# Sums of w3's halves on the tensor engine, and a second-layer group begun inside the last product of its input

## The chip, the cores and the metric

The kernel runs on one core of one Trainium2 chip. The time is device microseconds of that core. Three runs of the kernel before took 1224.52, 1227.14 and 1231.71 us; the median, 1227.14 us, is the time that the change is compared with. The profile is one further execution.

## The reference

Inputs are q, k, v of shape (8, 8, 576, 64) and two feed-forward layers. In short:

```python
# attention inside chunks of 64 tokens, per head
s = q_c @ k_c.T / sqrt(64); a = softmax(s); x = a @ v_c      # -> x: 4608 x 512
# layer 1
h = x @ w_in                 # 512 -> 2048
x = (h * sigmoid(h)) @ w_out # 2048 -> 512
# layer 2
h = x @ w_in2                # 512 -> 1024
e = exp(h - max(h)); solu = h * e / (sum(e) + 1e-9)
ln = (solu - mean) / sqrt(var + 1e-6) * g_ln
out = ln @ w_out2            # 1024 -> 512
```

All of it is float32.

## The kernel before

**Numbers.** Every float32 operand is kept as a float16 high half and a float16 low half (`split`, L105: ACT writes the high half, DVE or POOL the low half as the difference). A product of two operands is three matmuls: high by high, high by low, low by high.

**Blocks.** 4608 tokens are nine blocks of 512 (b = 0 to 8), each four tiles of 128 tokens. Attention of block b+1 is worked beside block b. A block runs in stages on PE (the tensor engine): H, the first layer's hidden values (w1, from x); X, the first layer's output (w2), which is the second layer's input; M, the second layer's hidden values (w3); then O, the output (w4).

**Seven products.** From b = 2 on, H, X and M cut each matrix product into 2 by 2 parts and take seven products in place of eight. Sums of the weights' quarters are wanted for that: w1's and w2's are made in block 1 (`w1_sums`, `w2_sums`, through `pe_sums`: PE adds high and low halves with an identity matrix, ACT and DVE finish), w3's in block 2 (`w3_sums`, L665, through `add_sums`, L368: DVE adds the halves, L371, and makes the sums, L372 to L375). `w3_sums` is called at steps 0 and 3 of block 2's X. `combine` (L486) walks the seven products in the order of its argument `seq`: PE accumulates in PSUM tiles pa, pb, pc; ACT copies some of them out (L496, L500, L503), DVE adds (`add`: L534 for H and X, L710 for M), and `done` is called for each quarter of the result as it is complete. For X, `done` (L596) splits the quarter (x2q), makes the four sums xt for M (L610 to L613), and splits those (x2s).

**Around the end of a block.** X's last product is j = 5, 48 matmuls 128x256 in four quarters of 12, one tile of streamed weights each (`x_product`, L574). The next block begins with M's group c = 0 (`m_fast(b - 1, 0)`; seven products of six matmuls 128x512, L696 to L698; tokens c = 0 want x2q and x2s of column c = 0 only), then its H. Group c = 1 comes in the middle of the next H stage. After M comes `m_norm`: maxima (nm, L749), exponentials (L752), normalisation (L754 to L772), a transposing DMA (L776).

**What sets the order.** The program is written in this order; a scheduler then orders instructions per engine by when they were written and what they need, so work of a later step can stand earlier on an engine. Each engine runs its list strictly in that order. All eight PSUM banks have one tag and go round. w1's and w2's products come through a ring of eight tiles of 256 KB (L440 to L457) that the SP queue loads, one load after each use; the same queue issues q, k and v (L170, L179) and the transposes. Names: q is the split hidden value of H, hc and xc are quarters of H and X, uT is the transposed normalised value, kb and qbh are k and q split for the scores, vbh and vbl the halves of v, s_ps the scores, x_ps the attention output, xf and xd its sums.

Of the kernel before, what the change touches and what calls it, by code (L numbers as in the profile page):

```python
# [12 lines left out]
ALU = mybir.AluOpType  # L13
# [3 lines left out]
P = 128  # L17
# [13 lines left out]
HB = BLK // 2  # L31
# [15 lines left out]
def fused(ctx: ExitStack, tc: tile.TileContext, qkv, w1, w2, w3, w4, g_ln, out):  # L47
    nc = tc.nc
    V, A, G, T = nc.vector, nc.scalar, nc.gpsimd, nc.tensor
# [13 lines left out]
    MO = (0, 1, 2, 3)  # L63
# [18 lines left out]
    for d in range(KD):  # L82
        for f in range(4):
            if f % 2 == 0:
                tag = f"w2_{2 * d + f // 2}" if d < 3 else f"q{12 + f // 2}"
                y = one.tile([P, 2, 2, 4, P], F16, tag=tag, name="w2t")
# [5 lines left out]
    w3q = {(n, k): one.tile([P, 2, 2, 512], F16, tag=f"w3_{n}{k}", name="w3q") for n in range(2) for k in range(2)}  # L92
# [63 lines left out]
    seq = [b * TPB + o for b in range(NB) for o in ORDER]  # L156
# [208 lines left out]

    def add_sums(ys, quads, engs):  # L368
        y11, y12, y21, y22 = ys
        for y, a, eng in zip(ys, quads, engs):  # L370
            eng.tensor_tensor(out=y, in0=a[:, 0], in1=a[:, 1], op=ALU.add)  # L371
        V.tensor_tensor(out=y22, in0=y21, in1=y22, op=ALU.add)  # L372
        V.tensor_tensor(out=y21, in0=y11, in1=y21, op=ALU.subtract)
        V.tensor_tensor(out=y11, in0=y22, in1=y11, op=ALU.subtract)
        V.tensor_tensor(out=y12, in0=y12, in1=y11, op=ALU.subtract)  # L375

    def pe_sums(ys, quads, y1122=None):

        n = 512 // P // quads[0].shape[2]

        def whole(qs):
            ps = [bank([P, n, 512 // n], "wq") for _ in range(len(qs) // n)]
            out = []
            for i, a in enumerate(qs):
                o = ps[i // n][:, i % n]
                for l in range(2):
                    T.matmul(o, ident16, a[:, l].rearrange("p a b -> p (a b)"), start=l == 0, stop=l == 1)
                out.append(o)
            return ps, out

        y11, y12, y21, y22 = (y.rearrange("p a b -> p (a b)") for y in ys)
        ps, o = whole([quads[0], quads[3]])
        if n == 2:
            A.activation(y1122, ps[0], AF.Copy)
        else:
            A.activation(y11, o[0], AF.Copy)
            A.activation(y22, o[1], AF.Copy)
        _, (p21, p12) = whole([quads[2], quads[1]])
        V.tensor_tensor(out=y22, in0=p21, in1=y22, op=ALU.add)
        V.tensor_tensor(out=y21, in0=y11, in1=p21, op=ALU.subtract)  # L400
        V.tensor_tensor(out=y11, in0=y22, in1=y11, op=ALU.subtract)
        V.tensor_tensor(out=y12, in0=p12, in1=y11, op=ALU.subtract)
# [9 lines left out]
            nc.sync.dma_start(out=dst(j), in_=z)  # L412

    sn = [0]
    E3, UL = (V, V, V, V), V

    def w1_sums(p):
        wa, wb = w1t[p], w1t[p + K1 // 2]
# [64 lines left out]
                T.matmul(ps[:, c], wl, x[:, 0, k], start=False, stop=k == 1, skip_group_check=True)  # L483
        ring.load()

    def combine(h, shape, seq, product, done, add):  # L486

        a, c = bank(shape, "pa"), {}
        for j in seq:
            if j == 0:
                product(j, a, True)
                A.activation(h[0], a, AF.Copy)  # L496
            elif j == 3:
                c[0] = bank(shape, "pb")
                product(j, c[0], True)
                A.activation(h[3], c[0], AF.Copy)  # L500
            elif j == 1:
                product(j, a, False)
                A.activation(h[1], a, AF.Copy)  # L503
            elif j == 4:
                p = bank(shape, "pc")
                product(j, p, True)
                add(0, h[0], p)
                done(0, 0, h[0])
            elif j == 2:
                product(j, a, False)  # L510
                add(3, h[3], a)
                done(1, 1, h[3])
            elif j == 6:
                product(j, c[0], False)
                add(1, h[1], c[0])
                if seq[-1] != 5:
                    done(1, 0, h[1])
            else:
                product(j, a, False)
                done(0, 1, a)  # L520
                if seq[-1] == 5:
                    done(1, 0, h[1])
            yield

    def run(*parts):

        parts = list(parts)
        while parts:
            for g in list(parts):
                if next(g, parts) is parts:  # L530
                    parts.remove(g)
# [39 lines left out]

        yield from combine(h, [P, 2, HB], HSEQ, lambda *a: h_product(b, *a), done, plain_add)

    def x_product(b, j, ps, start):  # L574
        for c in range(2):
            for q in range(2):
                w = ring.take()
                for f in range(4):
                    wh, wl = w[:, 0, f], w[:, 1, f]
                    g = qt[b, j, q][:, :, f]  # L580
                    first = start and c + q + f == 0
                    T.matmul(ps[:, c], wh, g[:, 0], start=first, stop=False, skip_group_check=True)  # L582
                    T.matmul(ps[:, c], wh, g[:, 1], start=False, stop=False, skip_group_check=True)  # L583
                    T.matmul(ps[:, c], wl, g[:, 0], start=False, stop=q == 1 and f == 3, skip_group_check=True)  # L584
                ring.load()

    def x_fast(b, step):
        h = [one.tile([P, 2, HB], F32, tag=f"w1_{12 + n}", name=f"xc{n}") for n in range(4)]

        def product(j, ps, start):  # L590
            step(XSEQ.index(j))
            x_product(b, j, ps, start)

        xs = {}

        def done(r, c, x):  # L596

            if (r, c) == (0, 1):
                A.activation(h[2], x, AF.Copy)
                x = h[2]  # L600
            scale = S_X2 / (S_G * S_W)
            n = HB if r else P
            y = one.tile([P, 2, 2, HB], F16, tag=f"x2_{2 * r + c}", name="x2q")
            split(y[:, 0, :, :n], y[:, 1, :, :n], x[:, :, :n], scale, A, V)
            xq[b, r, c] = y
            xs[r, c] = x
            if (0, c) in xs and (1, c) in xs:
                (a1, b1), (a2, b2) = ((xs[i, c][:, :, 0:P], xs[i, c][:, :, P:HB]) for i in range(2))
                t = one.tile([P, 4, 2, P], F32, tag=f"q{8 + c}", name="xt")
                TX.tensor_tensor(out=t[:, 0], in0=b1, in1=a1, op=ALU.subtract)  # L610
                TX.tensor_tensor(out=t[:, 2], in0=b2, in1=b1, op=ALU.subtract)
                TX.tensor_tensor(out=t[:, 1], in0=b2, in1=t[:, 0], op=ALU.subtract)
                TX.tensor_tensor(out=t[:, 3], in0=a2, in1=t[:, 1], op=ALU.subtract)  # L613
                z = [one.tile([P, 4, 2, P], F16, tag=f"w1_{8 + 2 * c + i}", name="x2s") for i in range(2)]
                split(*z, t, scale, A, V)
                xq[b, 2, c] = z

        run(combine(h, [P, 2, HB], XSEQ, product, done, plain_add))

    more_ = lambda b: b + 1 < NB  # L620
    TX = V
# [43 lines left out]
    def w3_sums(k):  # L665

        if not w3s:
            for j, n in ((1, 0), (2, 1), (3, 2), (5, 3)):
                w3s[j] = one.tile([P, 2, 2, 512], F16, tag=f"w2_{n}", name="w3s")
            w3s[0], w3s[4], w3s[6] = w3q[0, 0], w3q[0, 1], w3q[1, 1]  # L670
        ys = [one.tile([P, 2, 512], F32, tag=f"w2_{4 + i}", name="y") for i in range(2)]
        y = [ys[i // 2][:, i % 2] for i in range(4)]
        add_sums(y, [w3q[n, i][:, :, k] for n in range(2) for i in range(2)], E3)
        for i, j in ((0, 1), (3, 2), (2, 3), (1, 5)):
            split(w3s[j][:, 0, k], w3s[j][:, 1, k], y[i], 1.0, A, G)

# [101 lines left out]
    def in_turn(*parts):  # L778
        for g in parts:
            yield from g  # L780
# [120 lines left out]
    for b in range(NB):  # L901
# [4 lines left out]
        for f in range(K1):  # L906
# [22 lines left out]
            elif f % 8 == 0:  # L929
                if f and more:  # L930
                    load_qk(m, ("w1_14", "w1_15"))
                    prep_qk(m, ahead=False)
                if b == FAST:
                    for n in range(2):
                        run(m_h(b - 1, MO[f // 4 + n], *(("m1", "m2"), ("w2_5", "w2_4"))[n % 2]))
                if f and b == FAST:
                    for n in range(2):
                        run(m_out(b - 1, MO[n]))
                elif b > FAST:
                    run(m_fast(b - 1, f // 8), in_turn(*(m_out(b - 1, MO[n]) for n in range(2) if f)))  # L940
                run(h_fast(b, f // 4), h_fast(b, f // 4 + 1))
        if b == 0:
            g_split(b, K1 - 1, GH)
# [37 lines left out]
        if b < FAST:  # L981
            for s in range(8):
                step(s)
                x_part(b, s // 2, s % 2)
        else:
            x_fast(b, step)

    b = NB - 1
    run(m_fast(b, 0, alt=True))
    run(m_fast(b, 1), in_turn(m_out(b - 1, MO[2], high=False), m_out(b - 1, MO[3])))  # L990
    for t in MO:
        run(m_out(b, t))
# [47 lines left out]
```

## Time and profile before

| | before |
|---|---|
| runs (us) | 1224.52, 1227.14, 1231.71 |
| profiled execution (us) | 1232.02 |
| span of the profile (us) | 1230.2 |
| mean granted clock of PE | 0.979 |
| PE busy | 1132.8 us, 92% |
| DVE busy | 915.6 us, 74% |
| ACT busy | 802.5 us, 65% |
| POOL busy | 247.9 us, 20% |

The span is the time from the first to the last instruction; 1.8 us lie around it. A row of the timeline gives a start in us, the duration, the engine, the line, the operation, what it writes and reads, and in brackets how long its engine had stood idle before it and what ended that. PE is the busiest engine, but the shares are means over stages that differ: block 2's X stage (382.6 to 449.8 us) is not like block 3's (519.3 to 572.3 us), though PE has the same products in both. A granted clock of 1.00 is the full 2.4 GHz, 0.50 is 1.2 GHz.

### The profile page before, as it was taken

Reading aid. Unit: us, or ns where it says so; the run is one execution under the profiler, and the core shown is the slowest. Engines: PE = TensorE matmul, PEld = TensorE weight load, DVE = VectorE, ACT = ScalarE, POOL = GpSimd, SP = SyncE. Lnnn points to the kernel's source line nnn. Section 1 sums busy time; section 2 is a strip of 40 time slices with the busy share of each in tenths; the row PEclk is TensorE's granted clock in tenths of the full one; section 3 lists DMA queues with packets and bytes.
Section 4 is the critical chain, followed back from the end, with each engine's and each line's share of the span. In section 5 each row is a group of like instructions: output and inputs, shape, how many; then the busy total and the mean of one; then the engine's idle time right before and its main releaser. Section 6 shows DMA issues by size and latency. Waiting matters only on the chain.

```text
span 1230.2 us, 23553 instructions
## 1 busy us (share of the span) xinstructions
PE 1132.8 (92%) x9020; PEld 768.9 (63%) x9020; DVE 915.6 (74%) x1646; ACT 802.5 (65%) x1471; POOL 247.9 (20%) x241
## 2 busy tenths in 40 slices
PE   4997889988998699998999899999999999999998
PEld 4444334444656567686778676767676667776863
DVE  6788986577677878688868886888688867876353
ACT  7777667676666558755875587558755775677253
POOL 3355423334101510032003200220021002100001
PEclk8898989999999899999999999999999999999999
DMA  8778643543534565666566655665566657764604
GB/s 293 247 242 229 194 131 112 168 137 115 140 114 159 149 177 155 183 195 189 155 180 198 189 155 179 191 197 155 159 210 197 155 134 211 187 154 117 211 26 111
DMA packets 205169, 209.18 MB, mean 170 GB/s; under 512 B 120192, under 2 KB 130432, under 8 KB 205056
## 3 DMA queue, kind: packets, MB, share of 16 engines
q1 hardware_dynamic: 205056, 207.68, 57.8%
q8 instruction: 70, 1.15, 0.4%
q14 instruction: 43, 0.35, 0.1%
HBM read 156.24 MB, written 24.12 MB: 147 GB/s over the span
## 4 chain that ended last, share of the span: by engine, by line
PE 33%; DVE 11%; ACT 5%; DMA 5%; issue 3%; SPq 1%; POOL 0%; POOLq 0%; ACTq 0%
PE o_ps L790 3%; PE o_ps L791 3%; PE o_ps L798 3%; PE pa L584 2%; PE pa L583 2%; PE pa L582 2%; DVE vbl L113 2%; DMA ring<-w1s 2%; PE pa L481 2%; PE pa L483 1%; PE pa L482 1%; SPq L776 1%; ACT u L760 1%; PE pa L696 1%; PE pa L698 1%
## 5 line engine op out<-in xcount | busy, mean ns | idle before, releaser
L113 DVE SCALAR_TENSOR_TENSOR q<-hc,q 128x512 f16<-128x512 f32 x196 | 139.4, 719 | 14.6 <-ACT q L108 13.2
L108 ACT ACTIVATE q<-hc 128x512 f16<-128x512 f32 x196 | 120.9, 626 | 37.2 <-DVE hc L569 12.0
L112 POOL TENSOR_TENSOR qbl<-qk,qbh 64x512 f16<-64x512 f32 x58 | 75.5, 1302 | 253.8 <-ACT qbh L108 207.9
L582 PE MATMUL pa<-q,ring 128*128 128x256 f16 x448 | 123.7, 276 | 0.0
L584 PE MATMUL pa<-q,ring 128*128 128x256 f16 x448 | 123.6, 276 | 0.0
L583 PE MATMUL pa<-q,ring 128*128 128x256 f16 x448 | 123.6, 276 | 0.0
L790 PE MATMUL o_ps<-w4h,uT 128*128 128x512 f16 x288 | 109.3, 379 | 1.7 <-DMA uT<-u 1.7
L791 PE MATMUL o_ps<-w4l,uT 128*128 128x512 f16 x288 | 109.2, 379 | 0.0
L767 POOL TENSOR_TENSOR c<-c,mhalf 128x2 f32<-128x2 f32 (+1 forms) x22 | 14.1, 640 | 426.6 <-DVE c L766 426.6
L482 PEld LDWEIGHTS <-ring 128*128 128x128 f16 x784 | 76.6, 98 | 21.1 <-issue 10.9
L481 PEld LDWEIGHTS <-ring 128*128 128x128 f16 x784 | 76.6, 98 | 18.7 <-DMA ring<-w1s 8.3
L584 PEld LDWEIGHTS <-ring 128*128 128x128 f16 x784 | 77.2, 98 | 9.5
L583 PEld LDWEIGHTS <-ring 128*128 128x128 f16 x784 | 77.2, 98 | 9.2
L582 PEld LDWEIGHTS <-ring 128*128 128x128 f16 x784 | 77.2, 98 | 9.1
L483 PEld LDWEIGHTS <-ring 128*128 128x128 f16 x784 | 76.6, 98 | 9.0
L752 ACT ACTIVATE u<-e,nm 128x1024 f32<-128x1024 f32 x28 | 32.2, 1150 | 59.7 <-DVE nm L749 59.7
L481 PE MATMUL pa<-xb,ring 128*128 128x256 f16 x224 | 61.1, 273 | 10.4 <-DMA ring<-w1s 5.3
L798 PE MATMUL o_ps<-w4h,uT 128*128 128x512 f16 x288 | 70.3, 379 | 0.0
L481 PE MATMUL pa<-x,ring 128*128 128x256 f16 x224 | 61.0, 273 | 4.7 <-ACT hc L496 2.9
L481 PE MATMUL pb<-x,ring 128*128 128x256 f16 x224 | 61.1, 273 | 0.2 <-DMA ring<-w1s 0.2
L582 PE MATMUL pb<-q,ring 128*128 128x256 f16 x224 | 61.1, 273 | 0.0
L584 PE MATMUL pb<-q,ring 128*128 128x256 f16 x224 | 61.1, 273 | 0.0
(268 smaller groups left out, 3511.4 us busy)
## 6 DMA issues: line engine op xcount, KB each, us to landing
ring<-w1s SPq DMA_DIRECT2D x196, 256.0 KB, 3.5
ring<-w2s SPq DMA_DIRECT2D x196, 256.0 KB, 3.8
wst<-w SPq DMA_DIRECT2D x48, 512.0 KB, 4.9
qk<-qkv SPq DMA_DIRECT2D x29, 512.0 KB, 3.8
vs<-qkv SPq DMA_DIRECT2D x36, 256.0 KB, 3.4
out<-o SPq DMA_DIRECT2D x36, 256.0 KB, 2.1
w1s<-ws SPq DMA_DIRECT2D x32, 128.0 KB, 1.8
w2s<-ws SPq DMA_DIRECT2D x16, 256.0 KB, 2.0
```

The source lines that it names most:

```text
L108: A.activation(dst_h, src, AF.Copy, scale=scale)
L112: return G.tensor_tensor(out=dst_l, in0=src, in1=dst_h, op=ALU.subtract).ins
L113: return V.scalar_tensor_tensor(out=dst_l, in0=src, scalar=scale, in1=dst_h, op0=ALU.mult, op1=ALU.subtract).ins
L481: T.matmul(ps[:, c], wh, x[:, 0, k], start=first, stop=False, skip_group_check=True)
L482: T.matmul(ps[:, c], wh, x[:, 1, k], start=False, stop=False, skip_group_check=True)
L483: T.matmul(ps[:, c], wl, x[:, 0, k], start=False, stop=k == 1, skip_group_check=True)
L582: T.matmul(ps[:, c], wh, g[:, 0], start=first, stop=False, skip_group_check=True)
L583: T.matmul(ps[:, c], wh, g[:, 1], start=False, stop=False, skip_group_check=True)
L584: T.matmul(ps[:, c], wl, g[:, 0], start=False, stop=q == 1 and f == 3, skip_group_check=True)
L790: T.matmul(ps, uh[:, k], w4h[:, k, :], start=k == 0, stop=False)
L791: T.matmul(ps, uh[:, k], w4l[:, k, :], start=False, stop=False)
L798: T.matmul(ps, ul[:, k], w4h[:, k, :], start=False, stop=k == K2 - 1)
```

## The change

Two things are changed. First, `w3_sums` uses `pe_sums`: the halves of w3's quarters are added by PE (two identity matmuls per quarter, 16 in all), ACT copies two of the four sums out of PSUM, and DVE makes the other combinations from PSUM and these. The function now takes tiles with or without a fourth dimension (`flat`). Second, `m_fast(b, 0)` is created before X of the same block, and X's last product advances it by one product after each of its four quarters (`beside`); its other three products run where the group stood, at the start of the next block. So that the operands are there, `combine` may call `done` for quarter (1, 0) right after product 6 (`c21_first`), which X does.

```diff
-    def add_sums(ys, quads, engs):
-        y11, y12, y21, y22 = ys
-        for y, a, eng in zip(ys, quads, engs):
-            eng.tensor_tensor(out=y, in0=a[:, 0], in1=a[:, 1], op=ALU.add)
-        V.tensor_tensor(out=y22, in0=y21, in1=y22, op=ALU.add)
-        V.tensor_tensor(out=y21, in0=y11, in1=y21, op=ALU.subtract)
-        V.tensor_tensor(out=y11, in0=y22, in1=y11, op=ALU.subtract)
-        V.tensor_tensor(out=y12, in0=y12, in1=y11, op=ALU.subtract)
+    def flat(a, keep):
+        if len(a.shape) == keep + 1:
+            return a
+        return a.rearrange("p l a b -> p l (a b)" if keep == 2 else "p a b -> p (a b)")
...
     def pe_sums(ys, quads, y1122=None):
-        n = 512 // P // quads[0].shape[2]
+        ys, quads = ([flat(a, k) for a in v] for v, k in ((ys, 1), (quads, 2)))
+        n = 512 // quads[0].shape[2]
...
-                    T.matmul(o, ident16, a[:, l].rearrange("p a b -> p (a b)"), start=l == 0, stop=l == 1)
+                    T.matmul(o, ident16, a[:, l], start=l == 0, stop=l == 1)
...
-    def combine(h, shape, seq, product, done, add):
+    def combine(h, shape, seq, product, done, add, c21_first=False):
...
             elif j == 6:
                 product(j, c[0], False)
                 add(1, h[1], c[0])
-                if seq[-1] != 5:
+                if c21_first:
                     done(1, 0, h[1])
             else:
                 product(j, a, False)
                 done(0, 1, a)
-                if seq[-1] == 5:
+                if not c21_first:
                     done(1, 0, h[1])
...
-    def x_product(b, j, ps, start):
+    def x_product(b, j, ps, start, beside=()):
...
                 ring.load()
+                next(iter(beside), None)
...
-    def x_fast(b, step):
+    def x_fast(b, step, beside):
...
-            x_product(b, j, ps, start)
+            x_product(b, j, ps, start, beside if j == XSEQ[-1] else ())
...
-        run(combine(h, [P, 2, HB], XSEQ, product, done, plain_add))
+        run(combine(h, [P, 2, HB], XSEQ, product, done, plain_add, c21_first=True))
...
-        add_sums(y, [w3q[n, i][:, :, k] for n in range(2) for i in range(2)], E3)
+        pe_sums(y, [w3q[n, i][:, :, k] for n in range(2) for i in range(2)])
...
-                    run(m_fast(b - 1, f // 8), in_turn(*(m_out(b - 1, MO[n]) for n in range(2) if f)))
+                    run(m_fast(b - 1, 1) if f else begun, in_turn(*(m_out(b - 1, MO[n]) for n in range(2) if f)))
...
-            x_fast(b, step)
+            begun = m_fast(b, 0, alt=not more)
+            x_fast(b, step, begun)
...
-    run(m_fast(b, 0, alt=True))
+    run(begun)
```

DVE's list in block 2's H stage, before: the first sums of w3 (L371, L372) stand between the last normalisation of block 1 (L772) and the adds of the H quarters (L534).

```order
L772 TENSOR_TENSOR u<-e,u 128x1024
L371 TENSOR_TENSOR y<-w3q 128x512 x2
L372 TENSOR_TENSOR y<-y 128x512
L534 TENSOR_TENSOR hc_3931<-pc,hc_3931 128x512
L534 TENSOR_TENSOR hc_3951<-pc,hc_3951 128x512
L534 TENSOR_TENSOR hc_3934<-pa,hc_3934 128x512
L113 SCALAR_TENSOR_TENSOR q<-hc_3931,q 128x512
L113 SCALAR_TENSOR_TENSOR q<-hc_3951,q 128x512
```

The same place now (line numbers of the changed kernel are up to two lower; L532 is the add of H quarters):

```order
L770 TENSOR_SCALAR e<-e,nmu,c 128x1024
L772 TENSOR_TENSOR u<-e,u 128x1024
L532 TENSOR_TENSOR hc_3931<-pc,hc_3931 128x512
L532 TENSOR_TENSOR hc_3951<-pc,hc_3951 128x512
L532 TENSOR_TENSOR hc_3934<-pa,hc_3934 128x512
L113 SCALAR_TENSOR_TENSOR q<-hc_3931,q 128x512
L113 SCALAR_TENSOR_TENSOR q<-hc_3951,q 128x512
```

The three instructions on w3 have left this place; DVE's first operation of the new sums (L397) stands behind the last split of q.

PE's list at the end of block 2's X now: after the second quarter of X's last product (L580 to L582, accumulating in pa) comes the second M product (L696 to L698, into pb), then X's third quarter.

```order
L582 LDWEIGHTS ring
L582 MATMUL pa<-q,ring 128x256
L696 LDWEIGHTS x2s
L696 MATMUL pb<-w3s,x2s 128x512
L697 LDWEIGHTS x2s
L697 MATMUL pb<-w3s,x2s 128x512
L698 LDWEIGHTS x2s
L698 MATMUL pb<-w3s,x2s 128x512
...
L580 LDWEIGHTS ring
L580 MATMUL pa<-q,ring 128x256
```

Before, all 48 matmuls of X's last product stood ahead of the first M product. Of M's seven products the first four (0, 3, 1, 4) now stand after X's first, second, third and last quarter, and 2, 6 and 5 behind them.

DVE's list at the end of block 3's X, before (x2s in the last row but two is the low half of the sums for c = 0):

```order
L612 TENSOR_TENSOR xt<-xc_5916,xt 128x256
L113 SCALAR_TENSOR_TENSOR x2q<-xc_5916,x2q 128x512
L333 TENSOR_TENSOR xd<-xf 128x256
L334 TENSOR_TENSOR xd<-xf 128x256
L335 TENSOR_TENSOR xd<-xf,xd 128x256
L613 TENSOR_TENSOR xt<-xc_5916,xt 128x256
L336 TENSOR_TENSOR xd<-xf,xd 128x256
L113 SCALAR_TENSOR_TENSOR vbl<-vs,vbh 64x8x64
L113 SCALAR_TENSOR_TENSOR x<-xd,x 128x4x128
L113 SCALAR_TENSOR_TENSOR x2s<-xt,x2s 128x1024
L113 SCALAR_TENSOR_TENSOR x<-xd,x 128x4x128
L113 SCALAR_TENSOR_TENSOR vbl<-vs,vbh 64x8x64
```

And now:

```order
L612 TENSOR_TENSOR xt<-xc_5936,xt 128x256
L113 SCALAR_TENSOR_TENSOR x2q<-xc_5936,x2q 128x512
L613 TENSOR_TENSOR xt<-xc_5936,xt 128x256
L333 TENSOR_TENSOR xd<-xf 128x256
L334 TENSOR_TENSOR xd<-xf 128x256
L335 TENSOR_TENSOR xd<-xf,xd 128x256
L113 SCALAR_TENSOR_TENSOR vbl<-vs,vbh 64x8x64
L113 SCALAR_TENSOR_TENSOR x2s<-xt,x2s 128x1024
L336 TENSOR_TENSOR xd<-xf,xd 128x256
L113 SCALAR_TENSOR_TENSOR x<-xd,x 128x4x128
L113 SCALAR_TENSOR_TENSOR vbl<-vs,vbh 64x8x64
L113 SCALAR_TENSOR_TENSOR x<-xd,x 128x4x128
```

The last sum of xt (L613) moves ahead of three operations on xd, and the low half of x2s ahead of L336 and the first split of x. On ACT the high half of x2s moves likewise, ahead of the first split of x (x<-xd) and of the second v (vbh<-vs), but stays behind the first v and xb<-xf. Behind these rows, M's first maximum (L710) now stands between x2q of c = 1 and L612 of c = 1; before it stood behind x2s of c = 1.

## Rows read from the trace of the kernel before

**Rows 1.** PE's waits from 360 us on: us in total, times, longest.
```profile
PE pa L696 <- DVE mp L710: 8.7, 5, 1.9
PE pa L696 <- ACT e L503: 7.4, 5, 1.7
PE pa L481 <- DMA ring<-w1s: 5.3, 5, 1.5
PE pa L481 <- DVE hc L534: 5.1, 3, 2.3
```

**Rows 2.** Busy time by stretch: PE, PEld, DVE, ACT, POOL, clock, DMA share, GB/s.
```profile
382.60:449.80 67.20, 55.75 (x579) 45.05 (x578) 58.34 (x94) 42.34 (x97) 23.43 (x19) 0.90 0.54 150
519.30:572.30 53.00, 52.79 (x579) 43.07 (x577) 46.27 (x80) 30.40 (x54) 13.44 (x12) 1.00 0.71 219
```

**Rows 3.** DVE's timeline in block 2's H: start, duration, what runs.
```profile
373.68 1.29 DVE L371 TENSOR_TENSOR y<-w3q 128x512 f32<-128x512 f16 x2 [7.07 <-DMA uT<-u]
```

**Rows 4.** PE's timeline in block 2's H.
```profile
377.55 0.27 PE L481 MATMUL pa<-xb,ring 128*128 128x256 f16 x1 [1.95 <-DVE hc L534]
...
381.32 0.27 PE L481 MATMUL pa<-xb,ring 128*128 128x256 f16 x1 [2.31 <-DVE hc L534]
```

**Rows 5.** Block 2's X: L371 (min, median, max ns), then POOL's and DVE's timeline.
```profile
L371 DVE TENSOR_TENSOR y<-w3q x8: 676/682/1637, 373.7 to 413.8; 128x512 f32<-128x512 f16 x8
...
417.51 2.77 POOL L112 TENSOR_TENSOR w3s<-y,w3s 128x512 f16<-128x512 f32 x2 [3.16 <-ACT w3s L108]
...
419.19 1.64 DVE L375 TENSOR_TENSOR y<-y 128x512 f32<-128x512 f32 x1
420.75 0.68 DVE L209 TENSOR_REDUCE am<-s_ps 128x8 f32<-128x512 f32 x1
```

**Rows 6.** PE's timeline in block 2's X.
```profile
426.20 0.21 PE L205 MATMUL s_ps<-kb,qbh 128*128 128x64 f16 x1 [9.29 <-ACT kb L108]
...
431.43 0.42 PE L583 MATMUL pa<-q,ring 128*128 128x256 f16 x1
```

**Rows 7.** The operations that are added, in block 1: min, median, max ns.
```profile
L387 PE MATMUL wq<-w2t,ident x32: 376/379/380, 252.5 to 300.6; 128*128 128x512 f16 x32
...
L397 ACT ACTIVATE y<-wq x4: 576/583/643, 258.3 to 301.1; 128x512 f32<-128x512 f32 x4
```

**Rows 8.** PE's timeline at the end of block 3's X.
```profile
567.05 0.27 PE L582 MATMUL pa<-q,ring 128*128 128x256 f16 x1
...
572.29 0.38 PE L696 MATMUL pa<-w3q,x2q 128*128 128x512 f16 x1
...
573.59 0.38 PE L696 MATMUL pb<-w3s,x2s 128*128 128x512 f16 x1
...
579.53 0.38 PE L696 MATMUL pa<-w3s,x2s 128*128 128x512 f16 x1 [1.65 <-ACT e L503]
...
583.98 0.38 PE L696 MATMUL pa<-w3s,x2q 128*128 128x512 f16 x1 [1.70 <-DVE mp L710]
...
585.27 0.27 PE L481 MATMUL pa<-xb,ring 128*128 128x256 f16 x1
```

**Rows 9.** ACT's timeline there.
```profile
570.28 0.40 ACT L108 ACTIVATE xb<-xf 128x256 f16<-128x256 f32 x1
...
571.89 1.04 ACT L108 ACTIVATE x2s<-xt 128x1024 f16<-128x1024 f32 x1
```

**Rows 10.** DVE's timeline there.
```profile
570.00 0.41 DVE L613 TENSOR_TENSOR xt<-xc,xt 128x256 f32<-128x256 f32 x1
...
572.97 1.23 DVE L113 SCALAR_TENSOR_TENSOR x2s<-xt,x2s 128x1024 f16<-128x1024 f32 x1 [0.25 <-ACT x2s L108]
...
581.65 1.67 DVE L113 SCALAR_TENSOR_TENSOR kb<-qk,kb 128x512 f16<-128x512 f32 x1 [1.27 <-ACT kb L108]
```

**Rows 11.** PE's timeline at the end of block 7's X.
```profile
1064.66 0.19 PE L250 MATMUL x_ps<-pT,vbh 128*128 128x64 f16 x1 [2.38 <-DMA pT<-ae]
...
1066.18 0.42 PE L584 MATMUL pa<-q,ring 128*128 128x256 f16 x1
```

More of the change, by code (lines that the diff above doesn't have):

```diff
@@ L386, in whole @@
                 for l in range(2):
-                    T.matmul(o, ident16, a[:, l].rearrange("p a b -> p (a b)"), start=l == 0, stop=l == 1)
+                    T.matmul(o, ident16, a[:, l], start=l == 0, stop=l == 1)
                 out.append(o)
             return ps, out
-        y11, y12, y21, y22 = (y.rearrange("p a b -> p (a b)") for y in ys)
+        y11, y12, y21, y22 = ys
         ps, o = whole([quads[0], quads[3]])
@@ L414, in fused @@
     sn = [0]
-    E3, UL = (V, V, V, V), V
+    UL = V
     def w1_sums(p):
```

## The prediction, made before the changed kernel ran

> **What bounds the kernel now.** I read PE's list of waits first, because PE is busy 92% of the span and every microsecond that it stands idle late in the program is a microsecond of the end. From 360 us on that list is short, and four entries hold most of it: one wait of 9.29 us of the scores for kb [rows 6]; ten waits of M products, 8.7 + 7.4 = 16.1 us in five blocks, 3.2 us a block; and three waits of H products for hc, 5.1 us [rows 1]. The reader is to see that the change touches just these places. The table by stretches then tells how far the first one reaches [rows 2]: block 2's X stage takes 67.20 us, block 3's 53.00 us, and PE is busy 52.79 us of the latter. Block 3's stage is PE's own length; block 2's has 14.20 us on top, with DVE at 58.34 us against 46.27 us and a mean clock of 0.90. So w3's sums are what DVE has there beyond the rest, 12.07 us of them, and they hold back the attention work queued behind them. The timelines say in which way:
>
> In block 2's H, DVE stands 7.07 us at the first sum of w3, for a transposed u whose space the sum's output takes; it begins at 373.68 us [rows 3]. The adds of H's quarters are queued behind it, and PE waits for them twice, 1.95 and 2.31 us, 4.26 us together [rows 4]. In block 2's X the other sums of w3 come in two lots. The same L371 takes 0.68 us at the median and up to 1.64 us, and the last L375 1.64 us; the maximum of a score tile (L209) is reached only at 420.75 us, right behind that [rows 5]. Exponentials and kb come behind it on ACT, and PE stands 9.29 us until 426.20 us; X's matmuls afterwards run 0.42 us each where they took 0.27 us, which is the lower clock [rows 6, 8].
>
> At a block's end (block 3 stands for five) X's last product begins at 567.05 us, M at 572.29 us, and the next H at 585.27 us: 18.22 us. Of these, 48 X matmuls are 5.24 us (572.29 - 567.05) and seven M products of 1.30 us (573.59 - 572.29) are 9.10 us, in sum 14.34 us; 1.65 + 1.70 us are waits of M, the rest small gaps [rows 8]. The first wait is for a copy of pa by ACT that is queued behind the split of the second column's sums, the second for a maximum on DVE that is queued behind kb, 1.67 us long from 581.65 us; M goes on at 583.98 us [rows 8, 10].
>
> **The change part by part.**
>
> *(a) w3's first sums leave the place before H's adds.* DVE's list no longer has the wait for u there, so the two waits of 4.26 us go. What comes next is the ring: PE takes tiles earlier, and the 256 KB loads have no more time than before. H's products wait for the ring five times, 5.3 us in sum, 1.5 us at most [rows 1]; spread over the seven blocks that have this stage that is 0.8 us, which I take (bounds 0 and 1.5). Gain 3.5 us.
>
> *(b) The sums in block 2's X.* Removed from DVE are sixteen operations, eight a call, of which thirteen stood in this stage; added are eight, all here: 46.27 + 8 x 0.68 = 51.7 us in place of 58.34 us [rows 2, 5], under PE's length of the stage. Added to PE are 16 matmuls 128x512. In a run they stand 0.216 us apart (1.30 us for six), 3.5 us in sum, all on the path, since PE bounds this stage; their own 379 ns [rows 7] would make it 6.1 us if nothing overlapped. Added to ACT are four copies of 0.583 us [rows 7], 2.3 us on an engine with 42.34 us of work in 67.20 us: hidden, and if the copies hold up a score tile they cost at most their 2.3 us. The sums also take four PSUM banks a call until DVE has read them; for that and for one late tile I take 0.5 us (bounds 0 and the 2.4 us that the longest wait for an attention tile took elsewhere [rows 11]). What goes is the 14.20 us. Gain 14.2 - 3.5 - 0.5 = 10.2 us; bounds 14.2 - 3.5 = 10.7 us, and 3 us if half of the delay stays.
>
> The sums were slow where POOL worked: the last L375 took its 1.64 us from 419.19 us, with POOL at low halves of w3s from 417.51 us on [rows 5]. The Trainium skill ("SBUF — State Buffer", section on SBUF's two separate sides) says that a DVE operation with two inputs in SBUF and a GpSimd operation hold one pair of ports in turn, and that the loser stands still until the other is through. The measured pair, 0.68 and 1.64 us, agrees. By that rule the new combinations, three of four with an input in PSUM, would escape it and cost DVE 0.68 us each; if they did not, eight of them would take 13.1 us, and DVE would have nothing left over. The sum above doesn't need either: it takes the 0.68 us, and the third rival has the other case.
>
> *(c) M inside X's last product.* PE now does 12 X matmuls (1.31 us), M0, 12 X, M3, and so on, so M3 is reached 2 x 1.31 + 1.30 = 3.92 us after X's last product begins, at 570.97 us on block 3's clock. M3 reads x2s. Before, ACT wrote its high half from 571.89 to 572.93 us and DVE its low half from 572.97 to 574.20 us [rows 9, 10]. Now the last xt (L613, before at 570.00 us) stands right behind x2q, some 1.0 us earlier, and the high half on ACT stands behind xb, which ended at 570.68 us. That puts the high half at 570.7 to 571.75 us and the low half at 571.8 to 573.0 us. M3's first two matmuls read the high half and wait 0.8 us; the third, at 572.2 us, reads the low half and waits 0.8 us more: 1.6 us in all (bounds: 0.3 us, and 2.8 us if x2s is not a bit earlier than before). X's third quarter stands behind M3 on PE and waits with it; nobody else waits for it sooner than before.
>
> The two old waits go: the copies for M2 and M6 have two whole quarters to be made, and M4 is over later. But M5 needs the maximum of M2's sum, and DVE has, between X's end and it, two sums (L610, L611), a split, M4's maximum (0.76 us) and two more sums: about 3.7 us, against 3.9 us until PE is at M5. Add the maximum itself (0.68 us): 0.5 us of waiting (bounds 0 and the old 1.70 us). So block 3's stretch becomes 14.34 + 1.6 + 0.5 = 16.4 us against 18.22 us. The normalisation of this group comes later relative to PE, because kb and the last L749 now stand behind more work, and the loads of q and k follow x2q's and xt's last reading; H's copies on ACT are queued behind the exponentials. I take 0.3 us at H for it (bounds 0 and 1.7 us, a kb's length).
>
> Net: 18.22 - 16.4 - 0.3 = 1.5 us in block 3, whose waits of 3.35 us are 0.13 us above the mean of 3.22 us: 1.4 us a block, 7.0 us for five. Block 7's M had no wait, because X ran at the lower clock and gave x2s the time; nothing there. Block 8 had none either and now has M3's wait and a later M of the second column: -0.5 us (0 to -2). Gain 6.5 us.
>
> **Sum.** 3.5 + 10.2 + 6.5 = 20.2 us. The profiled execution took 1232.02 us (its span and 1.8 us around it) and would take 1211.8 us; the median of the runs lies 4.9 us below the profiled one, so I take the same saving from it: 1227.14 - 20.2 = 1206.9 us, rounded to 1207 us.
>
> **Rivals.**
>
> 1. *x2s takes the place of the old waits.* If x2s is ready no earlier than before, M3 waits 2.8 us and a block saves 18.2 - 17.6 - 0.3 = 0.3 us: (c) is 1.0 us, and the time 1227.1 - 3.5 - 10.2 - 1.0 = 1212 us. For it: ACT and DVE were without a gap just before x2s [rows 9, 10]. Against it: the order of three operations changes in x2s's favour.
>
> 2. *Everything pays.* x2s is ready when M3 comes, and no wait replaces the old ones: 3.9 us a block (18.22 - 14.34), less the 0.13 us each, five times, less block 8's 0.5: 18.3 us, and 1227.1 - 4.3 - 10.7 - 18.3 = 1194 us. Against it: DVE's 0.41 us steps between x2q and x2s are a chain that I see no cover for.
>
> 3. *w3's sums still hold block 2's attention.* If the score tile is late by half of what it was, or the new combinations are as slow as L375's 1.64 us [rows 5], (b) gives 3 us, and the time is 1227.1 - 3.5 - 3 - 6.5 = 1214 us. For it: DVE would be at 52 to 59 us of a stage of 56.5 us, without room for a late chain; against it, most of the excess was one wait of 9.29 us.
>
> 4. *The next H pays.* The exponentials of the group come later, and H's first copies on ACT wait behind them: 1.3 us more a block in seven blocks, 9 us, and 1216 us. For it: kb stands before the maximum on DVE in the trace and costs 1.67 us [rows 10].
>
> 5. *Slower.* M3 stands in PE's list ahead of X's own third quarter. If x2s's low half comes so late that PE is idle about as long as at block 7's end (2.38 us, after which 17 matmuls ran 0.42 us instead of 0.27 us, some 1.7 us [rows 11]), each of seven blocks loses the wait and the clock. A block then takes 14.34 + (T - 4.35) + 0.5 + 0.3 + 1.7 us, with T the low half's time after X's last product began (7.15 us before, 5.95 us by my count) and 4.35 us when M3's third matmul wants it. Over seven blocks this eats the 13.7 us of (a) and (b) if a block is 2.0 us longer than the 18.2 us now: T = 7.7 us, and at T = 8.7 us the kernel is 7 us slower (3.0 x 7 - 13.7), 1234 us. For it: the low half waits on three engines and on v's load. Against it: T would have to be later than before, though three operations that stood before it are now behind it. The Trainium skill ("TensorE: Matmul & The Clock Gate", "Step-by-step: what each phase is for") says that only weight loads are pulled ahead and matmuls stay in program order. The trace agrees: nothing of H ran in the 1.65 us before 579.53 us [rows 8]. By it X's quarter can't pass M3.
>
> **How the numbers follow.** My forecast, 1202 to 1210 us: 0.47. Rival 1: 0.14. Rival 2: 0.10. Rival 3: 0.12. Rival 4: 0.07. Two rivals together, or one of them with a lost (a), at 1217 to 1230 us: 0.06. Rival 5: 0.04. The range goes from 1197 to 1216 us and leaves out most of the last two, half of rival 2 and a little of rivals 3 and 4. Half a per cent, 6.1 us, is what a measurement of this kernel can tell from no change; below 1221 us lie all cases but rival 5 and most of the mixed one: faster 0.90, same 0.06, slower 0.04.
>
> **What would show it.** Right: no wait in H before 382 us; block 2's X near 57 us at full clock; the ten M waits gone from PE's list and in their place one of about 0.8 to 1.5 us for x2s in X's last product, in blocks 2 to 6; 16.4 us from that product's start to H in block 3. Wrong: a wait for kb or s_ps in block 2 over 3 us; M3 waiting 2.5 us or more, with slow X matmuls behind it; new waits at H for hc longer than 1 us.

## The result and the profile after

The changed kernel takes 1209.24 us (median of four runs, 1208.74 to 1211.81) where the kernel before took 1227.51 us beside it; the ratio is 0.9853, with a 95% interval from 0.9821 to 0.9885, so 18.0 us are saved (14 to 22). 1207 us was forecast, in a range from 1197 to 1216.

PE's waits from 360 us on, after the change (us in total, times, longest); they answer to [rows 1]:

```profile
PE pa L479 <- DMA ring<-w1s: 7.6, 6, 1.9
PE pb L698 <- DVE x2s L113: 4.1, 7, 0.8
PE x_ps L250 <- DMA pT<-ae: 3.2, 4, 1.3
PE pb L696 <- ACT x2s L108: 1.9, 2, 1.7
PE o_ps L790 <- DMA uT<-u: 1.7, 1, 1.7
PE x_ps L252 <- DVE vbl L113: 1.6, 2, 1.4
PE pa L479 <- DVE hc L532: 1.4, 5, 0.3
```

The ten M waits of 16.1 us are gone, and so are the 9.29 us for kb and the two long waits for hc. In their place stand waits of M3 for x2s, 6.0 us, and the ring's waits are 7.6 us where they were 5.3 us (3.3 us in a second profile of the kernel before).

Block 2 from the first matmul of the output in its H stage to the first of the next H, one row for each of three profiles: the kernel before, a second profile of the kernel before, the changed kernel. Columns as in [rows 2].

```profile
382.63:461.74 79.11, 65.08 (x621) 49.11 (x619) 67.22 (x110) 48.29 (x107) 25.73 (x21) 0.91 0.51 144
```
```profile
384.54:461.50 76.96, 65.37 (x620) 49.18 (x619) 65.61 (x109) 47.31 (x105) 25.91 (x21) 0.92 0.52 148
```
```profile
380.46:449.88 69.42, 65.94 (x637) 48.85 (x635) 58.63 (x100) 46.36 (x105) 24.32 (x20) 1.00 0.57 168
```

The stretch lost 9.69 us against the first profile and 7.54 us against the second; DVE fell by 8.6 us (67.22 to 58.63), PE gained 16 matmuls, and the clock is full.

The last product of block 3's X after the change (PE), for [rows 8]; it begins at 555.36 us, and H at 571.05 us:

```profile
559.71 0.39 PE L696 MATMUL pb<-w3s,x2s 128*128 128x512 f16 x1 [0.27 <-ACT x2s L108]
...
560.97 0.39 PE L698 MATMUL pb<-w3s,x2s 128*128 128x512 f16 x1 [0.65 <-DVE x2s L113]
...
571.05 0.27 PE L479 MATMUL pa<-xb,ring 128*128 128x256 f16 x1
```

15.69 us in place of 18.22 us (585.27 less 567.05 us [rows 8]). The waits of 0.27 and 0.65 us are the two that were forecast for M3, at 0.8 each; M5 waits for nothing.

The span, taken apart by the starts of PE's stages (each by its first matmul, in us; the last row goes to the end of the span; the second profile of the kernel before stands beside the first):

| stretch | before | before, 2nd | after | change | forecast |
|---|---|---|---|---|---|
| up to block 2's H | 316.38 | 317.55 | 318.71 | +2.3 | 0 |
| block 2, H to its output matmuls (a) | 66.25 | 66.98 | 61.75 | -4.5 | -3.5 |
| block 2, output to X's last product (b) | 61.90 | 59.89 | 54.26 | -7.6 | -10.2 |
| X's last product to H, blocks 2 to 6 (c) | 89.81 | 88.79 | 80.25 | -9.6 | -8.4 |
| H, blocks 3 to 8 | 378.97 | 377.20 | 380.27 | +1.3 | +1.5 |
| X up to its last product, blocks 3 to 6 | 168.93 | 171.40 | 168.55 | -0.4 | 0 |
| block 7, X to the next H | 60.03 | 57.44 | 57.72 | -2.3 | 0 |
| block 8, X and the end | 87.96 | 87.96 | 88.52 | +0.6 | +0.5 |

### The profile page after: what moved, and what is told of

Read it like the earlier page. It is cut to its first block, busy times and chain, and to the rows that moved or that the text cites. A ratio compares the mean times of both kernels' runs of the same rounds, so it can differ in the third digit from the quotient of the medians.

```text
span 1210.0 us, 23575 instructions
## 1 busy us (share of the span) xinstructions
PE 1137.6 (94%) x9036; PEld 770.7 (64%) x9036; DVE 906.0 (75%) x1638; ACT 805.5 (67%) x1475; POOL 251.8 (21%) x241
## 5 line engine op out<-in xcount | busy, mean ns | idle before, releaser
L112 POOL TENSOR_TENSOR qbl<-qk,qbh 64x512 f16<-64x512 f32 x58 | 79.7, 1374 | 283.0 <-ACT qbh L108 237.0
L580 PE MATMUL pa<-q,ring 128*128 128x256 f16 x448 | 122.7, 274 | 0.0
L582 PE MATMUL pa<-q,ring 128*128 128x256 f16 x448 | 122.7, 274 | 0.0
L580 PEld LDWEIGHTS <-ring 128*128 128x128 f16 x784 | 76.9, 98 | 11.3
L582 PEld LDWEIGHTS <-ring 128*128 128x128 f16 x784 | 76.9, 98 | 9.2
L479 PE MATMUL pa<-x,ring 128*128 128x256 f16 x224 | 61.3, 274 | 2.1 <-ACT hc L494 2.1
L481 PE MATMUL pa<-x,ring 128*128 128x256 f16 x224 | 61.5, 274 | 0.0
L480 PE MATMUL pa<-x,ring 128*128 128x256 f16 x224 | 61.3, 274 | 0.0
L580 PE MATMUL pb<-q,ring 128*128 128x256 f16 x224 | 61.1, 273 | 0.0
```

The lines of the kernel that those rows point to most:

```text
L112: return G.tensor_tensor(out=dst_l, in0=src, in1=dst_h, op=ALU.subtract).ins
L479: T.matmul(ps[:, c], wh, x[:, 0, k], start=first, stop=False, skip_group_check=True)
L480: T.matmul(ps[:, c], wh, x[:, 1, k], start=False, stop=False, skip_group_check=True)
```

## The experiments

Each is timed on one chip with the kernel before beside it (five runs or more), save two that were run once. The ratio is to the kernel before. A saving against the changed kernel is the difference of two such ratios from separate timings, and is uncertain by some 5 us.

**The w3 part alone.** The changed kernel with M begun where it was:

```diff
-        run(combine(h, [P, 2, HB], XSEQ, product, done, plain_add, c21_first=True))
+        run(combine(h, [P, 2, HB], XSEQ, product, done, plain_add))
...
-                    run(m_fast(b - 1, 1) if f else begun, in_turn(*(m_out(b - 1, MO[n]) for n in range(2) if f)))
+                    run(m_fast(b - 1, f // 8), in_turn(*(m_out(b - 1, MO[n]) for n in range(2) if f)))
...
-            begun = m_fast(b, 0, alt=not more)
-            x_fast(b, step, begun)
+            x_fast(b, step, ())
...
-    run(begun)
+    run(m_fast(b, 0, alt=True))
```

> The w3 part alone: w3's halves added by TensorE, M begun only after X as before. Account A (both parts pay, the first by the end of the DVE queue in block 2, 13.7 us by the forecast, the second by the M waits, 6.5 us): 1227.5 - 13.7 = about 1214 us (1212 to 1217); in the profile no wait for hc before 382 us, block 2's X stage near 58 us, and the ten M waits of 16 us still there. Rival B (the w3 part brings all, M inside X only moves the waits): 1209 to 1211 us. Rival C (w3's part brings little and the M part most): 1221 us or more.

**The M part alone.** The changed kernel with DVE's sums in `w3_sums` (`add_sums` is put back as it was):

```diff
-        pe_sums(y, [w3q[n, i][:, :, k] for n in range(2) for i in range(2)])
+        add_sums(y, [w3q[n, i][:, :, k] for n in range(2) for i in range(2)], E3)
```

> The M part alone: DVE adds w3's halves as before, M's first group is begun inside X's last product. Account A: 1227.5 - 6.5 = 1221 us (1218 to 1222), the waits of 9.3 us for kb and of 4.3 us for hc in block 2 still there, M's waits gone. Rival B: 1226 to 1228 us. Rival C: 1212 to 1215 us. If the two parts add up, the savings of this kernel and of the one with the w3 part alone are together the 18.3 us of the whole change, within 2 us; if they hide each other, more.

Measured: 1217.87 us, 0.9932 (0.9905 to 0.9958), for the w3 part: 8.3 us (5 to 12). 1215.29 us, 0.9921 (0.9901 to 0.9942), for the M part: 9.7 us (7 to 12). Together they are 18.0 us, the whole change, and within their intervals the parts add up. Rival B lies outside both intervals; rival C lies outside that of the M part, though the w3 part alone, at the low end of its interval, would not shut it out. The w3 part is worth less than the 13.7 us of the forecast and the M part more than its 6.5 us. PE's waits from 310 us on, with the w3 part alone and then with the M part alone:

```profile
PE pa L696 <- DVE mp L710: 8.1, 5, 1.8
PE pa L696 <- ACT e L501: 7.4, 5, 1.7
```
```profile
PE s_ps L205 <- ACT kb L108: 7.4, 1, 7.4
PE pb L707 <- DVE x2s L113: 5.0, 7, 1.0
...
PE pa L488 <- DVE hc L541: 3.8, 6, 1.7
```

Each part leaves the other's waits standing, as account A says, save that with the M part alone one of the two long waits for hc in block 2's H is left, 1.7 us, not both.

**w3's first sums behind H's splits.** The kernel before with one change of order (`lastq` holds DVE's last split of q in H; the lines that fill it are left out here):

```diff
-                w3_sums(W3S.index(s))
+                with tc.issue_after(lastq[0]):
+                    w3_sums(W3S.index(s))
```

> The kernel before, with the first call's sums of w3 (DVE as before) queued behind the last split of H's hidden values instead of ahead of H's adds. Account A (the wait for u at the head of DVE's queue made H wait): the waits of 1.95 and 2.31 us go, three operations of 1.9 us come into block 2's X, where kb is then as late or later (9.3 to 11 us): 1223.5 to 1226 us. Rival (H is held by something else there, the ring or ACT): the waits stay under another name, 1227 us. Rival (position is all that mattered in X too): kb's wait goes as well, 1214 us.

Measured: 1222.81 us, 0.9973 (0.9958 to 0.9987), 3.3 us. No wait for an hc that DVE adds is left in block 2's H, and kb is still late:

```profile
PE s_ps L205 <- ACT kb L108: 7.5, 1, 7.5
```

So step (a) is shown by itself, at 3.3 us (1.6 to 5.1): the place in the queue cost it, not the operations, which DVE still does. The queue in X is a second matter.

**A second profile of the kernel before.**

> The kernel before once more, for a second profile. If the first profile's block 2 is typical: the wait for kb 9.3 us, X's stage of block 2 73.2 us from its first to the next H's first matmul, 316.4 us until block 2's H. If it was a long one: kb's wait near 7.4 us, as in the two kernels that kept DVE's sums.

One run, 1229.0 us. Its wait for kb:

```profile
PE s_ps L205 <- ACT kb L108: 7.0, 1, 7.0
```

The 9.29 us of the first profile [rows 6] was a long one; with DVE's sums and POOL's low halves four profiles show 9.3, 7.0, 7.4 and 7.5 us.

**w3's low halves on DVE.** The kernel before, POOL relieved:

```diff
-            split(w3s[j][:, 0, k], w3s[j][:, 1, k], y[i], 1.0, A, G)
+            split(w3s[j][:, 0, k], w3s[j][:, 1, k], y[i], 1.0, A, V)
```

> The kernel before, with the low halves of w3's sums written by DVE in place of POOL. If DVE's sums of two operands in SBUF were slow because POOL worked beside them: L371 to L375 all at about 0.68 us, save beside POOL's halves of q (qbl), none at 1.64 us beside w3s; DVE has eight operations of 0.6 to 0.7 us more, so block 2's X stage is 0 to 3 us longer. If they were slow for another reason: still 1.5 to 1.6 us for some of them.

One run, 1217.97 us (nine runs of the kernel before beside it: 1223.09 to 1228.5). L375 in the kernel before, and here (count: min, median, max ns), and then the timeline of its slow one and of POOL beside it:

```profile
L375 DVE TENSOR_TENSOR y<-y x2: 1635/1637/1639, 408.0 to 419.2; 128x512 f32<-128x512 f32 x2
```
```profile
L375 DVE TENSOR_TENSOR y<-y x2: 676/950/1225, 405.0 to 415.5; 128x512 f32<-128x512 f32 x2
```
```profile
415.49 1.23 DVE L375 TENSOR_TENSOR y<-y 128x512 f32<-128x512 f32 x1
...
415.02 2.71 POOL L112 TENSOR_TENSOR qbl<-qk,qbh 64x512 f16<-64x512 f32 x2 [13.52 <-ACT qbh L108]
```

With POOL idle a sum takes 0.68 us; the one slow L375 that is left, and one L371 of 1.64 us at 400.41 us, lie beside POOL's halves of q. It was POOL that made DVE's sums long. The forecast that block 2's X would be no shorter was wrong: it was 69.1 us from its first matmul to the next H against 70.4 and 73.2 us. PE's waits for kb, high half and low:

```profile
PE s_ps L206 <- DVE kb L113: 2.5, 1, 2.5
PE s_ps L205 <- ACT kb L108: 1.4, 1, 1.4
```

The wait of 7.0 to 9.3 us for kb's high half is down to 1.4 us, though DVE has more to do than before. Steps (a) and (b) of the table are 121.1 us in this profile, against 128.2 and 126.9 us before and 115.1 us with the w3 part alone: about half of what that part takes out of block 2 comes by relieving POOL alone, with the sums still on DVE. It is one run and one profile, so this is no firm size.

**v's split late.** In the changed kernel, x2s's high half is queued on ACT behind the split of v for the next block, which waits for v's load. The experiment queues that split behind the next H's exponentials:

```diff
-                prep_v(m)
+                if b > FAST:
+                    with tc.issue_after(exps[-1]):
+                        prep_v(m)
+                else:
+                    prep_v(m)
```

> The changed kernel, with the first split of v of the next block (vbh, which waits for v's load) queued on ACT behind the exponentials of the next H stage instead of ahead of the high half of x2s. Theory D (after the change, M3 inside X waits for x2s because ACT's queue waits for v's load): the high half begins at L613's end, about 0.9 us earlier, and block 5's wait of 1.66 us with the half clock behind it goes: about 0.6 us a block and 3 us in block 5, 1204 to 1207 us. Rival E (DVE's own chain sets x2s): same waits of 0.4 to 0.8 us for DVE, 1208 to 1210 us. Rival F (v late holds up the attention of the next block): waits for vbl or vbh in X, over 1210 us.

Measured: 1200.53 us, 0.9791 (0.9766 to 0.9816). About 7.6 us less than the changed kernel by the ratios, more than expected, and mostly not for the reason given. M3's waits for the low half did not fall; the ring's did. PE's waits from 310 us on:

```profile
PE pb L698 <- DVE x2s L113: 5.7, 7, 1.1
...
PE pa L479 <- DMA ring<-w1s: 0.6, 1, 0.6
```

As to x2s rival E was right (DVE's chain sets the low half). Theory D could hold for block 5 alone, whose story is below; its stretch is 15.57 us here, but 15.72 us also with the M part alone, where v's split stands where it stood, so this is not shown. The ring's waits had to be explained anew. SP's queue in the changed kernel's block 4 and PE's wait for what it loads:

```profile
618.54 5.30 SPq L776 DMA_TRANSPOSE uT<-u  x4
623.93 0.53 SPq L449 DMA_DIRECT2D ring<-w1s  x1
...
627.11 0.28 PE L479 MATMUL pa<-xb,ring 128*128 128x256 f16 x1 [0.69 <-DMA ring<-w1s]
```

The last w1 tile of an H stage is issued behind four transposes, and PE is at it 3.2 us after the issue. Queueing v late moves v's load in SP's list and, with it, one ring load ahead of the transposes.

**The ring ahead.** The changed kernel, with v's split where it was:

```diff
-                nc.sync.dma_start(out=t, in_=src)
+                with tc.high_priority(offset=400):
+                    nc.sync.dma_start(out=t, in_=src)
```

> The changed kernel with the ring's loads given priority in SP's queue, so that the last w1 tile of an H stage stands behind one transposed u instead of four; v's first split stays ahead of x2s on ACT. Theory G (what queueing v late saved was the ring wait of H's last product, whose load stands behind the four transposes in SP's queue, 7.6 us in six waits): these waits go or fall under 0.4 us each, x2s's waits stay, 1202 to 1205 us. Rival D (the saving came from ACT's queue, x2s earlier): no more than 1 us, 1208 to 1210 us. Rival H (transposes later hold up the second layer's output): waits for uT, 1210 us or more.

Measured: 1197.34 us, 0.9782 (0.9761 to 0.9803). SP's queue at the same place of block 4, and PE's waits from 310 us on:

```profile
612.47 1.24 SPq L777 DMA_TRANSPOSE uT<-u  x1
613.80 0.53 SPq L450 DMA_DIRECT2D ring<-w1s  x1
```
```profile
PE pb L699 <- DVE x2s L113: 3.4, 6, 0.7
...
PE pb L697 <- ACT x2s L108: 2.0, 3, 1.2
```

No wait for the ring is left, x2s's waits stay at 5.4 us, and the time is 8.7 us below the changed kernel's by the ratios: theory G. In the profile the H stages of blocks 3 to 8 fell from 380.3 to 371.8 us; the six waits of 7.6 us were most of that price.

**M's products in another order.** In `m_fast` the order of X's products, so that M4, which reads x2q only, is the second inside X:

```diff
-        yield from combine(y, [P, 512], HSEQ, product, done, add)
+        yield from combine(y, [P, 512], XSEQ, product, done, add)
```

> The changed kernel with M's products in the order 0, 4, 1, 3, 2, 6, 5, so that the second one inside X reads x2q (there early) and x2s is wanted one quarter and one product later, 6.5 instead of 3.9 us after X's last product began. If M's wait for x2s inside X is still a price (4.1 + 4.8 us in the profile, block 5's half clock beside it): these waits go and the time falls by 5 to 7 us to 1202 to 1205 us. Rival (the time saved is spent in the ring wait at the end of H, which DMA sets): waits go, ring waits grow by as much, 1208 to 1210 us. Rival (the maxima come later): waits of M5 for a maximum, 0.5 to 1.5 us a block, 1206 us or more.

Measured: 1200.29 us, 0.9807 (0.9783 to 0.9832), 5.6 us less than the changed kernel by the ratios. No M product waits any more, and from X's last product to H every block takes 14.3 us, the forecast's 14.34 us without waits. A part is given back in H, and the ring's waits stay (PE's waits from 310 us on):

```profile
PE pa L479 <- ACT hc L501: 4.7, 6, 1.0
PE pa L479 <- DMA ring<-w1s: 4.3, 5, 1.6
```

**Two and three together.**

> Both orders: v's first split of the next block late, and M's products in the order 0, 4, 1, 3, 2, 6, 5. If the ring waits and the x2s waits are two separate prices, their savings add: 1200.5 - 5 = 1194 to 1197 us. If one feeds the other: 1199 to 1202 us.

> The changed kernel with M's products in the order 0, 4, 1, 3, 2, 6, 5 and the ring's loads with priority in SP's queue. If both prices are separate (ring wait of H's last product, about 11 us against the changed kernel; x2s's wait, about 6 us): 1191 to 1195 us, no wait for the ring over 0.4 us and none for x2s. If the second is hidden by the first: 1196 to 1198 us.

> The same with v's first split of the next block late on ACT as well. With M's products in the new order x2s is not waited for, and the ring's load already stands ahead, so late v has nothing left to save: the same as without it within 2 us. If v's place in ACT's queue has a price of its own: 3 us or more faster.

Measured: order of M and v late 1193.87 us, 0.9750 (0.9727 to 0.9772); order of M and ring ahead 1193.46 us, 0.9746 (0.9722 to 0.9771); all three 1192.41 us, 0.9729 (0.9709 to 0.9748). The prices of the ring and of x2s are mostly separate (13.1 us together against the changed kernel, 8.7 and 5.6 us singly), and v late adds nothing that can be told apart from the ring ahead. The last is the fastest: 33 us below the kernel before, 15 us below the changed one.

## Why the prediction was right, and where it was not

**The place and the sign.** The stretches that were named carry the change, by the mechanisms named: (a) by experiment, (b) and (c) by undoing each. The total came within 2.2 us because two terms were off in opposite ways, and that is luck. One of the signs failed: a wait of 2.13 us stands in block 2's H at 327.55 us, for a copy by ACT. It was there before (2.39 us at 325.49 us) and the change does not touch it.

**(a), 3.5 us.** 4.5 us between the profiles, 3.3 us (1.6 to 5.1) by its own experiment. The 4.5 us are rough, since PE's clock differed in this stage (last section). The 0.8 us set aside for the ring was not paid in block 2 (one wait of 0.22 us), but the ring is waited for in every H stage after it, which is part of the table's +1.3 us.

**(b), 10.2 us: the mis-sized term.** "What goes is the 14.20 us" took the difference of two stages from one profile, and in that profile kb's wait was 2 us longer than in the three others with DVE's sums and POOL's low halves. And of the 0.5 us for late tiles, 2.9 us were paid: 1.42 and 0.16 us for vbl, 1.33 us for a transposed pT. With the 5.24 us of X's last product the stage of [rows 2] thus takes 59.5 us, where 57 us was forecast. Between the profiles 7.6 us came, against the second profile of before 5.6 us; the whole w3 part, forecast at 13.7 us, is 8.3 us (5 to 12). The 16 matmuls cost what was said: eight of them stand from 386.33 to 388.06 us, 0.216 us each. The 12.07 us that DVE had beyond block 3 were in part POOL's doing (w3's low halves on DVE, above), which the forecast named and left out of its sum.

DVE's new sums were slow only where both operands lay in SBUF. The timeline of DVE, then POOL, in block 2's X after the change:

```profile
400.52 2.65 DVE L399 TENSOR_TENSOR y<-y 128x512 f32<-128x512 f32 x1
...
404.13 0.68 DVE L400 TENSOR_TENSOR y<-wq,y 128x512 f32<-128x512 f32 x1
...
421.32 0.69 DVE L400 TENSOR_TENSOR y<-wq,y 128x512 f32<-128x512 f32 x1
...
401.47 1.15 POOL L112 TENSOR_TENSOR w3s<-y,w3s 128x512 f16<-128x512 f32 x1
...
420.56 5.47 POOL L112 TENSOR_TENSOR w3s<-y,w3s 128x512 f16<-128x512 f32 x4 [0.35 <-ACT w3s L108]
```

L399, the one sum of two operands in SBUF, took 2.65 us beside POOL; L400, with one operand in PSUM, 0.69 us in the middle of POOL's 5.47 us. The Trainium skill ("SBUF — State Buffer", section on SBUF's two separate sides) says just this of a DVE operation with two SBUF inputs, and the trace agrees; the seven others of the eight took 0.68 to 0.69 us, among them the second L399, which began at 420.52 us, 0.04 us before POOL did.

**(c), 6.5 us: right in kind, too small.** The M part is 9.7 us (7 to 12) by its own run. Block 3's stretch is 15.69 us instead of the 16.4 us forecast: M3 waits 0.92 us, not 1.6, since x2s's low half began 4.33 us after X's last product did, where 4.75 us was reckoned; and M5's 0.5 us wasn't paid at all. DVE's row:

```profile
559.69 1.23 DVE L113 SCALAR_TENSOR_TENSOR x2s<-xt,x2s 128x1024 f16<-128x1024 f32 x1 [0.39 <-ACT x2s L108]
```

The 0.3 us at H were paid (five waits for hc of 0.25 to 0.33 us). Block 8's 0.5 us were 0.6 us.

**The slower rival happened once.** In block 5 the stretch took 18.75 us, longer than the 17.99 us before. ACT's queue and then PE's there:

```profile
802.18 0.63 ACT L108 ACTIVATE vbh<-vs 64x512 f16<-64x512 f32 x1 [2.39 <-DMA vs<-qkv]
...
803.03 1.04 ACT L108 ACTIVATE x2s<-xt 128x1024 f16<-128x1024 f32 x1
```
```profile
804.12 0.39 PE L696 MATMUL pb<-w3s,x2s 128*128 128x512 f16 x1 [1.66 <-ACT x2s L108]
...
805.38 0.39 PE L698 MATMUL pb<-w3s,x2s 128*128 128x512 f16 x1 [0.66 <-DVE x2s L113]
...
806.71 0.42 PE L581 MATMUL pa<-q,ring 128*128 128x256 f16 x1
```

v's load landed late, x2s stood behind it on ACT, PE waited 1.66 and 0.66 us, and X's matmuls then ran 0.42 us each. x2s's low half, begun at 804.10 us and 1.23 us long, was ready 6.95 us after X's last product had begun at 798.38 us: earlier than the 7.7 us at which this rival was to eat the gain. The forecast named v's load as the risk and asked for one idle stretch of about 2.4 us; two of 2.3 us together were enough here. (At block 7's end before, 15 matmuls ran 0.42 us, and one on either side of them 0.38 and 0.32 us; the forecast counted 17 at 0.42 us.) This is one profile: with the M part alone block 5's stretch is 15.72 us. v's load was issued no later than elsewhere; from its issue to ACT's split 4.8 us passed (797.35 to 802.18 us), where it was 3.5 us in block 3 (554.27 to 557.77 us).

**What the forecast did not see.** The ring's wait at the end of H was taken as a cost that comes with a faster PE, and set down once, at 0.8 us for block 2. It is an order in SP's queue, was there before the change (5.3 us [rows 1], 3.3 us in the second profile), is 7.6 us after it, and goes when the ring's loads are queued ahead of the transposes. And [rows 11], block 7's wait of 2.38 us with its half clock, is not a fixture: in the second profile of the kernel before that stage takes 57.4 us, not 60.0.

Still open: how the w3 part's 8.3 us split between kb's wait, the clock behind it and POOL's hold on DVE's sums, and why v's load took longer in block 5.

## What to carry to other kernels

Before a stall is counted as a gain, look at it in a second profile: the largest single wait is the likeliest to be a long sample. When a product is pulled into another's stream, list what its operands still wait for, and let the product that needs the latest operand come last; here the order of the products was worth another 5.6 us beside the move's 9.7 us. After a stall is gone, read the queue that issues the loads, in its order: a load whose issue stands behind four transposes, 5.3 us of them, looks like slow memory. And when a DVE operation of two SBUF operands is longer in one place than in another, see what POOL does beside it before DVE's work is moved.

## What the runs showed of the hardware that was not expected

In ten profiles whose programs are the same up to block 2's H, that H began at 314.8 to 318.9 us: 4.1 us of difference without a cause in the program, as much as step (a) was worth. PE's clock fell to its lower level after two waits of 1.66 and 0.66 us with two matmuls between them, and stayed full after 1.65 and 1.70 us with a dozen between them [rows 8]. One and the same wait can go either way: early in block 2's H all 13 profiles have PE wait 1.9 to 2.4 us for ACT's copy of hc; the clock fell soon after it in ten of them (after 2.13 us in the changed kernel, with a granted clock of 0.50 from 328.2 to 331.5 us) and stayed full in three (after 2.39 us in the kernel before).
